# Weaving the bursts of two token pairs and moving three tiles' routing marks in a three-stage kernel

## The chip, the cores and the metric

The kernel runs on one core of a Trainium2 chip. The core has five engines with an instruction stream each: PE (TensorE, matrix products and transposes, with PEld its weight loads), DVE (VectorE), ACT (ScalarE), POOL (GpSimd) and SP (SyncE, which issues DMAs here). They run side by side and wait for each other on semaphores. The metric is the device time of one execution in microseconds (us); shown are the median, the lowest and the highest of several runs.

## The reference

Three layers follow each other: an attention with a window and block summaries, a dense mixture of four experts, and a mixture of eight experts in which each token goes to one expert at most and keeps its input beside it. There are 1536 tokens of 512 values, which the kernel holds as 12 tiles of 128 tokens.

```python
def _attn_ref(q, k, v):                    # q, k, v: (2, 8, 768, 64)
    block, window = (32, 16)
    k_sum = k.reshape(B, H, nb, block, D).max(axis=3)
    v_sum = v.reshape(B, H, nb, block, D).mean(axis=3)
    scores_l = scale * np.matmul(q, k.transpose(0, 1, 3, 2))
    mask_l = np.abs(pos[:, None] - pos[None, :]) < window
    scores_s = scale * np.einsum('bhsd,bhnd->bhsn', q, k_sum) + np.log(block)
    ...                                    # softmax over both, times v and v_sum

def _moe_ref(x, domain_probs, w1, w2):     # N, D, E, F = 1536, 512, 4, 1024
    p = domain_probs / (domain_probs.sum(-1, keepdims=True) + 1e-09)
    for e in range(E):
        h = np.maximum(x @ w1[e], 0.0)
        out += p[:, e:e + 1] * (h @ w2[e])

def _moe2_ref(x, w_skip, w_gate, w1, w2):  # E = 8
    do_compute = x @ w_skip > 0
    xc = x[do_compute]
    logits = xc @ w_gate
    e_idx = np.argmax(logits, axis=1)
    gate_w = probs[np.arange(len(xc)), e_idx]          # probs: softmax of logits
    y[mask] = gate_w[mask, None] * (np.maximum(xc[mask] @ w1[e], 0.0) @ w2[e])   # mask: e_idx == e
    out[do_compute] = xc + y
```

## The kernel before

**Stages.** From 0 to about 203 us run the attention and the first groups of the dense mixture, in an order that a scheduler makes. Then the order is the written one (`manual_schedule`, L1339): the function `middle` (L576) runs ten weight groups up to about 527 us; the last two groups run block by block up to 608 us (blocks of 4, 3, 3 and 2 token tiles), with the routing of the third layer between their products; and from there to the end the third layer runs in slots of 128 gathered tokens.

**Precision.** A product of full precision is built of three products of split values: each operand has a high part (cast) and a low part (what the cast left over), and high·high, high·low and low·high are summed in a PSUM bank. In names, `h` and `l` at the end are these parts. After the first matrix product `hh` is the relu of a bank, made by ACT, and `hl` its low part, made by DVE (L369, L370); both are needed by the second product (L382).

**The middle.** A weight group is a quarter of one expert's hidden width: 256 rows. The tokens are taken in two pairs of halves, pair "l" (tiles 4 to 11, 512 columns) and pair "s" (tiles 0 to 3, 256 columns). For each pair the 2×2 block product (weights by tokens) is made by seven products of sums instead of eight; each is a *burst* of six matmuls in one go (L509). They are called p1, p5, p6, p3, p7, p2, p4 and add up in three banks, with copies by ACT (the sums `u2` and `s5`) and additions by DVE (L544, L549) in between. Then the second product makes one *tile* of 128 tokens at a time (`second`, L560: six matmuls, then one DVE operation L570 onto the accumulator `acc`). Tiles are put into a list, `todo`, and one is taken from it behind nearly each burst; the list runs over into the next group. The table `at` (L583) says behind which burst the next group's weights are loaded, summed (POOL) and split (ACT casts, DVE subtractions). So a group has 14 bursts and 12 tiles.

**The routing.** `route_block` (L673) returns, for a block of token tiles, a list of routing steps and a list `place`. The steps store and transpose the block, make the logits, and `ranks` gives each token a place in its expert's list, which it counts on in `cum` (L752). In `place`, `places` *marks* (L759): a token's place is compared with all 640 places of the lists, one DVE operation per tile; `index` (L783) multiplies these marks with the token numbers and adds to `iacc` (L788). The steps go into a queue `rq` (L1413), and each small unit of the last groups' products pops one (L1404). What `rq` still holds is done in slot "x" with the last block's own list `r` (L1441): `slot_main` (L1040) takes one step behind each of its products (`step`). The last block's list contains its own `ranks`, `index(0, 1)` followed by the first gather, marks for the other places and the rest of `index`; behind these comes `first_trans` (L1437), which transposes the first gathered rows.

Of the kernel before, what the change touches and what calls it, by code (L numbers as in the profile page):

```python
# [19 lines left out]
P = 128  # L20
# [4 lines left out]
def attention_moe_kernel(  # L25
# [5 lines left out]
    B, S, _ = v.shape  # L31
    H, D = 8, q.shape[3]
    NT, DM = out.shape
    E1, NG, _, _ = w1.shape
# [13 lines left out]
    bank = [psp.tile([P, 512], F32, name=f"bank{i}") for i in range(8)]  # L48
# [357 lines left out]
    SGROUPS = range(4, E1 * NG - 2)  # L406

    PAIRS = {"l": (4 * P, 4 * P), "s": (0, 2 * P)}
    xsum, scr = {}, {}

    def x_quarter(p, i, j, c=slice(0, 2)):

        n0, n = PAIRS[p]
        return [x[:, 2 * i + c.start : 2 * i + c.stop, :] for x in x_at(n0 + j * n, n)]
# [39 lines left out]
    def w_steps(g):  # L454

        mid = g in SGROUPS

        def sums():
            raw = wtiles[g][0][0].rearrange("p (c f) -> p c f", c=KC)
            a11, a12, a21, a22 = (raw[:, 2 * j : 2 * j + 2, i * P : (i + 1) * P] for i in range(2) for j in range(2))  # L460
            t = scr["w"].tile([P, 3, 2, P], F32, name=f"ws{g}", tag="ws")
            tt = nc.gpsimd.tensor_tensor
            tt(out=t[:, 1], in0=a11, in1=a21, op=ALU.subtract)  # L463
            tt(out=a21, in0=a21, in1=a22, op=ALU.add)
            tt(out=t[:, 0], in0=a21, in1=a11, op=ALU.subtract)
            tt(out=t[:, 2], in0=a12, in1=t[:, 0], op=ALU.subtract)
            parts = [scr["w"].tile([P, 3, 2, P], F32R, name=f"ws{n}{g}", tag=f"ws{n}{g % 2}") for n in "hl"]
            wtiles[g] += [parts, t]

        def sum_parts(i):  # L470
            (h, l), t = wtiles[g][3:]
            s = slice(0, 2) if i == 0 else slice(2, 3)
            nc.scalar.copy(h[:, s], t[:, s])
            nc.vector.tensor_sub(l[:, s], t[:, s], h[:, s].bitcast(F32))  # L474

        no = lambda: None
        return [
            lambda: load_w(g), sums if mid else no, lambda: split_w(g, 1), lambda: split_w(g, 0),
            (lambda: sum_parts(0)) if mid else no, (lambda: sum_parts(1)) if mid else no,
            lambda: split_w(g, 2), lambda: split_w(g, 3),  # L480
        ]

    def pair_work(g, p, state_):

        n0, n = PAIRS[p]
        w1h, w1l = wtiles[g][1]
        wsh, wsl = wtiles[g][3]
        e = g // NG
        ba, be, bb = bank[state_["i"] % 2], bank[6], bank[7 - 2 * (state_["i"] % 2)]
        state_["i"] += 1  # L490
        hs, fs = {}, {}

        def wq(i, j):
            return [[w[:, (2 * j + c) * GF + i * P : (2 * j + c) * GF + (i + 1) * P] for w in (w1h, w1l)] for c in range(2)]

        def wsum(k):
            return [[w[:, k, c, :] for w in (wsh, wsl)] for c in range(2)]

        def xq(i, j):
            h, l = x_quarter(p, i, j)  # L500
            return [[x[:, c, :] for x in (h, l)] for c in range(2)]

        def xs(k):
            return [[x[:, k, c, :] for x in xsum[p]] for c in range(2)]

        def burst(b, w, x, start):
            for c in range(2):
                for i, (a, m) in enumerate(((0, 0), (0, 1), (1, 0))):
                    nc.tensor.matmul(  # L509
                        b[:, :n], w[c][a], x[c][m], start=start and c == 0 and i == 0, stop=c == 1 and i == 2,  # L510
                        skip_group_check=True,
                    )

        def tmp(nm):
            t = fs[nm] = scr["w"].tile([P, n], F32, name=f"{nm}{p}{g}", tag=f"{nm}{p}")
            return t

        def part(i, j, src):
            if p == "l" and j == 1:
                pool, tag = hp_, ("hh", "hl")  # L520
            else:
                pool, tag = scr["h"], (f"hh{p}{i}{j}", f"hl{p}{i}{j}")
            hh, hl = (pool.tile([P, n], F32R, name=f"{t}_{p}{g}_{i}{j}", tag=t) for t in tag)
            nc.scalar.activation(hh, src, AF.Relu)
            nc.vector.scalar_tensor_tensor(
                out=hl, in0=src, scalar=0.0, in1=hh.bitcast(F32), op0=ALU.max, op1=ALU.subtract,
            )
            hs[i, j] = (hh, hl)

        def p1():  # L530
            burst(ba, wq(0, 0), xq(0, 0), True)
            nc.scalar.copy(bb[:, :n], ba[:, :n])

        def p5():
            burst(be, wq(1, 0), xs(0), True)
            nc.scalar.copy(tmp("s5"), be[:, :n])

        def p6():
            burst(bb, wsum(0), xs(1), False)
            nc.scalar.copy(tmp("u2"), bb[:, :n])  # L540

        def p3():
            burst(be, wsum(2), xq(1, 1), False)
            nc.vector.tensor_add(fs["u2"], be[:, :n], fs["u2"])  # L544
            part(0, 1, fs["u2"])

        def p7():
            burst(bb, wsum(1), xs(2), False)
            nc.vector.tensor_add(fs["s5"], bb[:, :n], fs["s5"])  # L549
            part(1, 1, fs["s5"])  # L550

        def p2():
            burst(ba, wq(0, 1), xq(1, 0), False)
            part(0, 0, ba[:, :n])

        def p4():
            burst(bb, wq(1, 1), xs(3), False)
            part(1, 0, bb[:, :n])

        def second(j, t):  # L560
            w2h, w2l = wtiles[g][2]
            b = bank[2 + state_["b"] % 3]
            state_["b"] += 1
            for i in range(2):
                hh, hl = (h[:, t * P : (t + 1) * P] for h in hs[i, j])
                s = slice(i * DM, (i + 1) * DM)
                for k_, (a, w) in enumerate(((hh, w2h), (hh, w2l), (hl, w2h))):
                    nc.tensor.matmul(b, a, w[:, s], start=i == 0 and k_ == 0, stop=i == 1 and k_ == 2)  # L568
            t_ = n0 // P + j * (n // P) + t
            nc.vector.scalar_tensor_tensor(  # L570
                out=acc[:, t_, :], in0=b, scalar=pr[:, t_, e : e + 1], in1=acc[:, t_, :], op0=ALU.mult, op1=ALU.add,
            )

        return [p1, p5, p6, p3, p7, p2, p4], [lambda j=j, t=t: second(j, t) for j in (1, 0) for t in range(n // P)]

    def middle(todo):  # L576

        todo = list(todo)
        state_ = dict(i=0, b=0)

        wh = wtiles[SGROUPS[0]][1][0]
        nc.tensor.matmul(bank[7], wh[:, :P], wh[:, :512], start=True, stop=True)
        at = {0: (0,), 2: (1,), 4: (2,), 5: (3,), 7: (4,), 8: (5,), 9: (6,), 11: (7,)}  # L583
        for g in SGROUPS:
            nxt = w_steps(g + 1)
            i = 0
            for p in "ls":
                bursts, tiles = pair_work(g, p, state_)
                for b in bursts:
                    b()  # L590
                    for k_ in at.get(i, ()):
                        nxt[k_]()
                    if i not in (9, 12) and todo:
                        todo.pop(0)()
                    i += 1
                todo += tiles
        return todo


# [688 lines left out]
    rq = []  # L1288
    rstack, sstack, tstack = ExitStack(), ExitStack(), ExitStack()
    prev = None  # L1290
# [33 lines left out]
    for ch in chunks:  # L1324
        first = ch["ci"] == 0
        p1 = ch["gs"][0] < 2
        g = ch["g"]
# [10 lines left out]
        if ch["gs"] == (last - 1,) and first and ch["t0"] == 0:  # L1338
            ctx.enter_context(tc.manual_schedule())  # L1339
            prev = dict(gs=(last - 2,), last=True, b=middle(prev["b"]))  # L1340
            load_w(last)
# [65 lines left out]
        if prev is not None and prev["gs"][-1] == last and prev["last"]:  # L1407
            r, place = route_block(prev["t0"], prev["nt"])
            if prev["t0"] == 0:
                r += [None] * 4 + [early_pick] + [None] * 2 + [early_weights]  # L1410
            if prev["t0"] == 4:
                r += [None] * 3 + [early_list] + [None] * 3 + [early_gather, early_close]
            rq += r + [None] * 1 + place  # L1413
        prev = ch
    for f in prev["b"]:
        f()
# [21 lines left out]
        xts[0] = slot_trans("0", gat[0][2], bank[0])  # L1438

    r, place = route_block(prev["t0"], prev["nt"])  # L1440
    r = [f for f in rq if f is not None] + r  # L1441
    r += [None] * (FT - len(r)) + [first_trans]
    free += [rbp.tile([P, FF], F32, name=f"rb{i}") for i in range(NRB)]
    load_units(5)
# [96 lines left out]
```

## Time and profile before

| | |
|---|---|
| median of 3 runs | 708.9 us (708.82 to 712.36) |
| the profiled execution | 707.44 us, span in the trace 705.7 us |
| mean granted TensorE clock in it | 0.992 of full speed |
| busy share of the span | PE 97%, DVE 60%, ACT 35%, POOL 15% |
| DMA | 73.78 MB, mean 105 GB/s |

A busy share is a mean over stages with different limits. The profiled execution is one of its own and stands a little apart from the median; the rows in the section below are all from it. "Idle before" in brackets is how long an engine stood still ahead of an instruction, and behind the arrow stands what it was waiting for. A granted clock of 1.00 is full speed and 0.50 half of it.

### The profile page before, as it was taken

The page shows a single profiled execution, that of the slowest core. Times are in us where ns is not written, and L with a number is a line of the kernel's source. Part 1 is how long each engine was busy: PE and PEld are TensorE (multiplying, and loading weights), DVE is VectorE, ACT ScalarE, POOL GpSimd, SP SyncE. Part 2 cuts the span into 40 slices and gives each one's busy share as a digit, 9 for nine tenths or more (in the row PEclk, how much of TensorE's full clock was granted, in tenths as well). Part 3 has the DMA queues.
Part 4 walks back from the last instruction along what each step waited for, and adds up shares of the span by engine and source line. Part 5 has one row for each costly group of instructions (what it writes and reads, how often), then busy time and mean ns, then how long its engine had stood idle before and what let it go on. Part 6 is the DMA issues. An engine that isn't in the chain of part 4 may idle for free. (4 is left out here: it accounts for less than half of the span.)

```text
span 705.7 us, 10995 instructions
## 1 busy us (share of the span) xinstructions
PE 686.7 (97%) x4072; PEld 547.7 (78%) x4072; DVE 425.5 (60%) x1035; ACT 245.5 (35%) x617; POOL 103.5 (15%) x182
## 2 busy tenths in 40 slices
PE   7889999999999999999999999999999999899996
PEld 6879888878888888888888888888888888474361
DVE  7877664897437565565657565565654565584441
ACT  4656564532114232332323233332311223271240
POOL 6117200020001010101101010100010003331230
PEclk9999999999999999999999999999999999899999
DMA  9977210020000010000000010000050187467991
GB/s 260 262 174 163 65 47 23 31 90 30 31 0 31 31 60 30 31 31 30 31 31 33 27 60 30 31 31 30 31 211 0 61 338 269 154 245 293 413 406 40
DMA packets 39877, 73.78 MB, mean 105 GB/s; under 512 B 16740, under 2 KB 19812, under 8 KB 39824
## 3 DMA queue, kind: packets, MB, share of 16 engines
q1 hardware_dynamic: 38592, 70.31, 30.3%
q0 software_dynamic: 960, 2.25, 0.9%
q8 instruction: 32, 0.52, 0.3%
q10 hardware_dynamic: 272, 0.52, 0.2%
q14 instruction: 21, 0.17, 0.1%
HBM read 66.10 MB, written 7.86 MB: 105 GB/s over the span
## 5 line engine op out<-in xcount | busy, mean ns | idle before, releaser
L570 DVE SCALAR_TENSOR_TENSOR acc<-bank,pr,acc 128x512 f32<-128x512 f32 x120 | 89.7, 747 | 61.1 <-PE bank L568 60.9
L362 PE MATMUL bank<-xh,w1h 128*128 128x256 f32 (+2 forms) x208 | 68.6, 334 | 0.0
L362 PE MATMUL bank<-xl,w1h 128*128 128x256 f32 (+2 forms) x208 | 67.7, 326 | 0.0
L362 PE MATMUL bank<-xh,w1l 128*128 128x256 f32 (+2 forms) x208 | 67.4, 324 | 0.0
L382 PE MATMUL bank<-w2h,hh 128*128 128x512 f32 x144 | 58.7, 408 | 0.0
L382 PE MATMUL bank<-w2h,hl 128*128 128x512 f32 x144 | 54.6, 403 | 4.3 <-DVE hl L370 4.3
L382 PE MATMUL bank<-w2l,hh 128*128 128x512 f32 x144 | 56.8, 394 | 0.0
L463 POOL TENSOR_TENSOR ws<-raw 128x256 f32<-128x256 f32 x10 | 7.5, 753 | 335.2 <-DVE wsl L474 195.4
L370 DVE SCALAR_TENSOR_TENSOR hl<-bank,hh 128x256 fp32r<-128x256 f32 (+2 forms) x52 | 27.0, 520 | 45.3 <-ACT hh L369 45.2
L369 ACT ACTIVATE hh<-bank 128x256 fp32r<-128x256 f32 (+2 forms) x52 | 24.1, 463 | 86.2 <-PE bank L362 84.1
L294 ACT ACTIVATE sm<-sm,mn 128x120 f32<-128x120 f32 x96 | 36.7, 385 | 19.9 <-DVE mn L289 19.9
L362 PEld LDWEIGHTS bank<-xh,w1h 128*128 128x128 f32 x208 | 39.1, 189 | 4.3 <-DVE hl L370 0.4
L362 PEld LDWEIGHTS bank<-xl,w1h 128*128 128x128 f32 x208 | 39.4, 189 | 3.3
L362 PEld LDWEIGHTS bank<-xh,w1l 128*128 128x128 f32 x208 | 39.3, 189 | 2.6
L392 DVE SCALAR_TENSOR_TENSOR acc<-bank,pr,acc 128x512 f32<-128x512 f32 x43 | 30.0, 743 | 17.9 <-PE bank L382 17.9
L382 PEld LDWEIGHTS bank<-w2h,hl 128*128 128x128 f32 x144 | 26.8, 189 | 11.6 <-DVE hl L370 6.2
L382 PEld LDWEIGHTS bank<-w2h,hh 128*128 128x128 f32 x144 | 27.3, 190 | 6.4 <-issue 2.3
L568 PE MATMUL bank<-w2h,hhl_l 128*128 128x512 f32 x80 | 31.8, 397 | 0.0
L568 PE MATMUL bank<-w2l,hhs_s 128*128 128x512 f32 x80 | 31.7, 396 | 0.0
L568 PE MATMUL bank<-w2l,hhl_l 128*128 128x512 f32 x80 | 31.6, 396 | 0.0
L568 PE MATMUL bank<-w2h,hh_l 128*128 128x512 f32 x80 | 31.6, 395 | 0.0
L568 PE MATMUL bank<-w2l,hh_l 128*128 128x512 f32 x80 | 31.6, 395 | 0.0
(357 smaller groups left out, 1731.5 us busy)
## 6 DMA issues: line engine op xcount, KB each, us to landing
raw<-in_moe_w_dram SPq DMA_DIRECT2D x30, 512.0 KB, 3.2
ra<-in_moe_w_dram SPq DMA_DIRECT2D x27, 512.0 KB, 9.1
rb<-in_moe_w_dram SPq DMA_DIRECT2D x21, 512.0 KB, 8.6
acc<-in_moe_w_dram SPq DMA_DIRECT2D x15, 512.0 KB, 8.5
vwin<-in_v_dram SPq DMA_DIRECT2D x24, 192.0 KB, 3.3
kt<-in_k_dram SPq DMA_DIRECT2D x8, 384.0 KB, 6.2
qbd<-in_q_dram SPq DMA_DIRECT2D x24, 128.0 KB, 6.3
out_dram<-xg SPq DMA_DIRECT2D x12, 256.0 KB, 3.0
```

Of the source, the lines that this page charges most:

```text
L294: nc.scalar.activation(sm[:, h, :], sm[:, h, :], AF.Exp, bias=mn[:, h : h + 1], scale=-1.0, accum_out=su[:, h : h + 1],)
L362: nc.tensor.matmul(b[:, :n], wt[:, f0 : f0 + P], xt[:, c, :], start=(c == 0 and i == 0), stop=(c == KC - 1 and i == 2),)
L369: nc.scalar.activation(hh[:, :n], b[:, :n], AF.Relu)
L370: nc.vector.scalar_tensor_tensor(out=hl[:, :n], in0=b[:, :n], scalar=0.0, in1=hh[:, :n].bitcast(F32), op0=ALU.max, op1=ALU.subtract,)
L382: nc.tensor.matmul(bank[2 + t], ht[:, t * P : (t + 1) * P], wt[:, f0 : f0 + DM], start=(ci == 0 and i == 0), stop=(ci == nch - 1 and i == 2),)
L392: nc.vector.scalar_tensor_tensor(out=a, in0=bank[2 + t], scalar=sc, in1=a, op0=ALU.mult, op1=ALU.add,)
L463: tt(out=t[:, 1], in0=a11, in1=a21, op=ALU.subtract)
L568: nc.tensor.matmul(b, a, w[:, s], start=i == 0 and k_ == 0, stop=i == 1 and k_ == 2)
L570: nc.vector.scalar_tensor_tensor(out=acc[:, t_, :], in0=b, scalar=pr[:, t_, e : e + 1], in1=acc[:, t_, :], op0=ALU.mult, op1=ALU.add,)
```

## The change

In the middle, the fourteen bursts of both pairs are issued woven together by a table, `order`, instead of all of pair l and then all of pair s; the steps of the next group's weights are put behind other bursts, and the tiles of pair l's second half enter the list behind the eleventh burst. In the routing, `place` of tiles 7 to 9 is no longer put into `rq`: its two steps of marks and its `index` are put between the first steps of the last block, in slot "x".

```diff
@@ pair_work
-        ba, be, bb = bank[state_["i"] % 2], bank[6], bank[7 - 2 * (state_["i"] % 2)]
-        state_["i"] += 1
+        ba, be, bb = (bank[i] for i in ((0, 6, 7) if p == "l" else (1, 6, 5)))
@@ middle
-        at = {0: (0,), 2: (1,), 4: (2,), 5: (3,), 7: (4,), 8: (5,), 9: (6,), 11: (7,)}
+        at = {0: (0,), 2: (1,), 3: (2,), 5: (3,), 7: (4,), 9: (5,), 10: (6,), 12: (7,)}
+        order = ("l1", "l5", "s1", "l6", "l3", "s6", "l7", "s5", "l2", "s7", "l4", "s3", "s2", "s4")
         for g in SGROUPS:
             nxt = w_steps(g + 1)
-            i = 0
-            for p in "ls":
-                bursts, tiles = pair_work(g, p, state_)
-                for b in bursts:
-                    b()
-                    for k_ in at.get(i, ()):
-                        nxt[k_]()
-                    if i not in (9, 12) and todo:
-                        todo.pop(0)()
-                    i += 1
-                todo += tiles
+            work = {p: pair_work(g, p, state_) for p in PAIRS}
+            for i, (p, k) in enumerate(order):
+                work[p][0][k]()
+                for k_ in at.get(i, ()):
+                    nxt[k_]()
+                if i == 10:
+                    todo += work["l"][1][0]
+                for _ in range(2 if g == SGROUPS[0] and i < 2 else i not in (9, 10)):
+                    if todo:
+                        todo.pop(0)()
+            todo += work["l"][1][1] + work["s"][1][0] + work["s"][1][1]
@@ where a block's steps are queued
-            rq += r + [None] * 1 + place
+            if prev["t0"] == 7:
+                late = [f for f in place if f is not None]
+                rq += r
+            else:
+                rq += r + [None] * 1 + place
@@ ahead of slot x
-    r = [f for f in rq if f is not None] + r
+    r = [f for f in rq if f is not None] + r[:1] + late[:1] + r[1:2] + late[1:2] + r[2:3] + late[2:] + r[4:]
```

Where instructions move, three places are shown. The first is ACT in the first group of the middle: `hh_l_11` is made of what l7 gives, `hhl_l_10` of what l4 gives; `u2s`, `s5s` and `hhs` belong to pair s. The kernel before, and then the changed one:

```order
L524 ACTIVATE hh_l_01_2295<-u2l_2275 128x512
L524 ACTIVATE hh_l_11_2310<-s5l_2263 128x512
L101 CAST w1h_2247<-raw_0_2249 128x512
L524 ACTIVATE hhl_l_00_2322<-bank_61 128x512
L101 CAST w1h_2247<-raw_0_2249 128x512
L524 ACTIVATE hhl_l_10_2334<-bank_68 128x512
L532 COPY bank_66<-bank_62 128x256
```

```order
L523 ACTIVATE hh_l_01_2308<-u2l_2297 128x512
L539 COPY u2s_2318<-bank_66 128x256
L101 CAST w1h_2247<-raw_0_2249 128x512
L523 ACTIVATE hh_l_11_2329<-s5l_2267 128x512
L535 COPY s5s_2339<-bank_67 128x256
L473 CAST wsh_2289<-ws_2284 128x512
L523 ACTIVATE hhl_l_00_2349<-bank_61 128x512
L523 ACTIVATE hhs_s_11_2360<-s5s_2339 128x256
L473 CAST wsh_2289<-ws_2284 128x256
L523 ACTIVATE hhl_l_10_2372<-bank_68 128x512
```

Between the results of l7 and l4 stood only the weight casts and the result of l2; now there are also the copy of s5 and the result of s7.

The second is DVE at the end of the last groups: `ofs` and `cum` close the ranks of tiles 7 to 9, `sel` are their marks, and `hl_10_1` is the low part that the last two tiles' second product needs; `ls` are the last block's logits. Before, and then after:

```order
L748 SCALAR_TENSOR_TENSOR ofs<-ix_5499,r_5559 128x3
L752 TENSOR_TENSOR cum<-cum,oh_5502 128x8 x3
L759 TENSOR_SCALAR sel_5573<-iot,ofs 128x640 x3
L370 SCALAR_TENSOR_TENSOR hl_10_1_5592<-bank_62,hh_10_1_5591 128x256
L392 SCALAR_TENSOR_TENSOR acc<-bank_63,pr,acc 128x512
L788 TENSOR_TENSOR iacc<-iacc,bank_66 128x25
L392 SCALAR_TENSOR_TENSOR acc<-bank_64,pr,acc 128x512
L718 COPY ls_5690<-bank_66 128x18
```

```order
L750 SCALAR_TENSOR_TENSOR ofs<-ix_5499,r_5559 128x3
L754 TENSOR_TENSOR cum<-cum,oh_5502 128x8 x3
L370 SCALAR_TENSOR_TENSOR hl_10_1_5590<-bank_62,hh_10_1_5589 128x256
L392 SCALAR_TENSOR_TENSOR acc<-bank_63,pr,acc 128x512
L392 SCALAR_TENSOR_TENSOR acc<-bank_64,pr,acc 128x512
L761 TENSOR_SCALAR sel_5661<-iot,ofs 128x640 x3
L720 COPY ls_5677<-bank_66 128x18
```

The three marks stood between the additions to `cum` and `hl_10_1`; now they stand behind both additions to `acc`, ahead of `ls`.

The third is PE at the start of slot x: L1065 (L1067 after) are the slot's own products, L694 (L696) the last block's transposes, L700 (L702) and L710 (L712) its logits. Before, and then after:

```order
L1065 MATMUL bank_62<-ra_4758,acc 128x512
L694 MATMUL bank_67<-ident,acc 128x128 x4
L694 MATMUL bank_68<-ident,acc 128x128 x4
L1065 MATMUL bank_62<-ra_4759,acc 128x512
L700 MATMUL bank_67<-rxt_5647,wr 32x256 x4
L1065 MATMUL bank_62<-ra_4760,acc 128x512
L710 MATMUL bank_66<-fold,lt_5685 128x9 x2
L1065 MATMUL bank_62<-ra_4761,acc 128x512
L1065 MATMUL bank_63<-ra_4758,acc 128x512
```

```order
L1067 MATMUL bank_62<-ra_4758,acc 128x512
L696 MATMUL bank_67<-ident,acc 128x128 x4
L696 MATMUL bank_68<-ident,acc 128x128 x4
L1067 MATMUL bank_62<-ra_4759,acc 128x512
L1067 MATMUL bank_62<-ra_4760,acc 128x512
L702 MATMUL bank_67<-rxt_5627,wr 32x256 x4
L1067 MATMUL bank_62<-ra_4761,acc 128x512
L1067 MATMUL bank_63<-ra_4758,acc 128x512
L712 MATMUL bank_66<-fold,lt_5669 128x9 x2
L1067 MATMUL bank_63<-ra_4759,acc 128x512
```

Each of the two logit steps now comes one product of the slot later than the step before it, since a step of marks has taken a place.

## Rows read from the trace of the kernel before

**Rows 1.** The page, part 1: engine busy time, share of the span, instructions.
```profile
PE 686.7 (97%) x4072; PEld 547.7 (78%) x4072; DVE 425.5 (60%) x1035; ACT 245.5 (35%) x617; POOL 103.5 (15%) x182
```

**Rows 2.** Waits of the weight loads (PEld), 200 to 527 us: line, releaser, total, times, longest.
```profile
PEld bank L509 <- DVE s5l L549: 0.5, 1, 0.5
```

**Rows 3.** Waits of PE, 527 to 706 us.
```profile
PE bank L382 <- DVE hl L370: 3.2, 1, 3.2
PE bank L821 <- DVE cum L752: 0.2, 1, 0.2
```

**Rows 4.** Timeline of PE: start us, us, engine, line, operation, shapes, count [idle before].
```profile
216.08 0.40 PE L509 MATMUL bank<-xh,w1l 128*128 128x512 f32 x1
216.50 0.50 PE L509 MATMUL bank<-xslh,w1h 128*128 128x512 f32 x1
216.84 0.40 PE L509 MATMUL bank<-xsll,w1h 128*128 128x512 f32 x1
```

**Rows 5.** Timeline of PE around the wait for hl.
```profile
602.46 0.39 PE L382 MATMUL bank<-w2l,hh 128*128 128x512 f32 x1
606.08 0.80 PE L382 MATMUL bank<-w2h,hl 128*128 128x512 f32 x1 [3.24 <-DVE hl L370]
```

**Rows 6.** Timeline of ACT, copies to u2l of the second and tenth group.
```profile
237.35 0.59 ACT L540 COPY u2l<-bank 128x512 f32<-128x512 f32 x1 [2.14 <-PE bank L509]
...
489.40 0.59 ACT L540 COPY u2l<-bank 128x512 f32<-128x512 f32 x1 [2.14 <-PE bank L509]
```

**Rows 7.** Windows: A:B, length, busy us (x instructions) of PE, PEld, DVE, ACT, POOL, PEclk, DMA share, GB/s.
```profile
145.00:200.00 55.00, 54.98 (x242) 44.84 (x240) 37.06 (x58) 13.81 (x24) 6.70 (x8) 1.00 0.11 39
```

**Rows 8.** Timeline of DVE from ranks' additions on, and in slot x.
```profile
601.68 1.61 DVE L752 TENSOR_TENSOR cum<-cum,oh 128x8 bf16<-128x8 bf16 x3
603.22 2.48 DVE L759 TENSOR_SCALAR sel<-iot,ofs 128x640 bf16<-128x640 f32 x3
605.62 0.40 DVE L370 SCALAR_TENSOR_TENSOR hl<-bank,hh 128x256 fp32r<-128x256 f32 x1
...
615.01 0.18 DVE L718 COPY ls<-bank 128x18 f32<-128x18 f32 x1 [5.45 <-PE bank L710]
...
617.46 0.35 DVE L752 TENSOR_TENSOR cum<-cum,oh 128x8 bf16<-128x8 bf16 x2
```

**Rows 9.** Timeline of POOL beside the additions to cum.
```profile
602.00 1.28 POOL L999 TENSOR_TENSOR sl<-ra,sh 128x512 fp32r<-128x512 f32 x1 [1.81 <-ACT sh L998]
```

**Rows 10.** Windows around three waits of PE.
```profile
48.80:52.20 3.40, 3.40 (x27) 3.07 (x27) 2.95 (x14) 2.26 (x10) 0.18 (x1) 0.50 0.26 63
135.00:140.00 5.00, 3.96 (x22) 2.87 (x22) 5.00 (x10) 2.94 (x7) 0.00 (x0) 1.00 0.33 105
605.20:612.00 6.80, 5.92 (x30) 4.18 (x31) 2.42 (x5) 0.59 (x1) 1.43 (x3) 0.50 0.39 125
```

**Rows 11.** Timeline of PE, two earlier waits.
```profile
47.39 0.65 PE L316 MATMUL bank<-ident,sm 128*120 128x128 f32 x4 [1.97 <-DVE xl L338]
...
139.81 0.73 PE L382 MATMUL bank<-w2h,hl 128*128 128x512 f32 x2 [0.85 <-DVE hl L370]
```

**Rows 12.** Timeline of PE in slot x.
```profile
618.13 1.02 PE L1065 MATMUL bank<-ra,acc 128*128 128x512 f32 x2
618.99 0.20 PE L783 MATMUL bank<-code,sel 128*128 128x5 bf16 x2
...
624.21 0.60 PE L1025 MATMUL bank<-ident,xg 128*128 128x128 f32 x4
```

**Rows 13.** Timeline of POOL, issue of the first gather.
```profile
620.18 1.10 POOL L1011 DMA_INDIRECT xg<-out_dram,ixb  x1 [1.67 <-DVE ixb L812]
```

**Rows 14.** Answer on tile xg, 585 to 706 us, its last line.
```profile
DMA to landing us min/median/max: 3.4/5.9/6.7
```

More of the change, by code (lines that the diff above doesn't have):

```diff
@@ L572, in second @@
             )
-        return [p1, p5, p6, p3, p7, p2, p4], [lambda j=j, t=t: second(j, t) for j in (1, 0) for t in range(n // P)]
+        bursts = {"1": p1, "5": p5, "6": p6, "3": p3, "7": p7, "2": p2, "4": p4}
+        return bursts, [[lambda j=j, t=t: second(j, t) for t in range(n // P)] for j in (1, 0)]
     def middle(todo):
         todo = list(todo)
-        state_ = dict(i=0, b=0)
+        state_ = dict(b=0)
         wh = wtiles[SGROUPS[0]][1][0]
         nc.tensor.matmul(bank[7], wh[:, :P], wh[:, :512], start=True, stop=True)
-        at = {0: (0,), 2: (1,), 4: (2,), 5: (3,), 7: (4,), 8: (5,), 9: (6,), 11: (7,)}
+        at = {0: (0,), 2: (1,), 3: (2,), 5: (3,), 7: (4,), 9: (5,), 10: (6,), 12: (7,)}
+        order = ("l1", "l5", "s1", "l6", "l3", "s6", "l7", "s5", "l2", "s7", "l4", "s3", "s2", "s4")
         for g in SGROUPS:
             nxt = w_steps(g + 1)
-            i = 0
-            for p in "ls":
-                bursts, tiles = pair_work(g, p, state_)
-                for b in bursts:
-                    b()
-                    for k_ in at.get(i, ()):
-                        nxt[k_]()
-                    if i not in (9, 12) and todo:
+            work = {p: pair_work(g, p, state_) for p in PAIRS}
[7 more added lines that the diff above has]
+                    if todo:
                         todo.pop(0)()
-                    i += 1
-                todo += tiles
+            todo += work["l"][1][1] + work["s"][1][0] + work["s"][1][1]
         return todo
```

## Prediction

> **What bounds the kernel now.** I read the page's busy shares first, then the waits of PE stretch by stretch, then the timelines around each wait. The shares show one engine full and the rest with room [rows 1]: PE is busy 97% of the span, DVE 60%, ACT 35%, POOL 15%. So the end is PE's own work plus whatever PE waits for. In the middle (200 to 527 us) the only wait is one of 0.5 us, a weight load held for DVE's addition to s5l [rows 2]. From 527 us to the end one wait stands out: an L382 product waits 3.2 us for DVE's hl [rows 3]. Two more things cost PE time without being a wait: the pace of the products in the middle, and a stretch behind that 3.2 us wait where the clock is halved. The change touches these four places and no other, since the first 203 us are issued as before.
>
> **Part one, the weave: first group.** Before, the first group runs out of leftover products, so l4 is issued one burst behind l7 while DVE still adds to s5l. The starts show it: 216.08, 216.50 and 216.84 [rows 4], so distances of 0.42 and 0.34 us where two products of 512 columns in a row stand 0.23 apart (602.23 to 602.46 [rows 5]); that is 0.30 us, the rest of the 0.5 lies at the same spot of the s pair. After, s5, l2 and s7 stand between l7 and l4: two bursts of six 256-column products and one of six 512-column ones, 12 × 0.12 + 6 × 0.23 = 2.8 us, and the addition is long done. Gain 0.5 us, at least 0 and at most 0.5.
>
> **Part one: later groups.** The bursts, the products behind them and the additions are the same in number. What can change is the distance from a burst that writes a bank to the burst that needs what DVE or ACT made of it. In the order before, the shortest was a product tile and one s burst (1.4 + 0.7 = 2.1 us, s5 to s3) and no group but the first shows a wait; after, the shortest such distance is l4, s3, a tile, s2 and a tile (s7 to s4), 5.6 us. The weight preparation, moved by a burst or two, is work of ACT, DVE and POOL, which have 65%, 40% and 85% of their time free; if that cover were gone it would show as a wait of tenths of a us in each of ten groups. I cost it at nothing.
>
> **Part one: pace.** A group takes 31.51 us: the copy to u2l starts at 237.35 in the second group and at 489.40 in the tenth, 252.05 / 8 [rows 6]. It holds 42 products of 512 columns and 42 of 256 in bursts and 72 of 512 in tiles, worth 135 of 512 columns. A uniform stretch issued 242 products in 55.00 us, 0.2273 each [rows 7]; 135 × 0.2273 = 30.7 us. So the middle runs 0.83 us a group above that pace, 8.3 us over ten groups, without a wait to show for it. I don't know the cause, and the weave mixes the widths more finely: from −8.3 (all of it goes) to +8.3 (as much again). The set of products and of operands stays the same, so I take 0.
>
> **Part two, the marks out of the way of hl.** Here lies most of the sum. PE could go on at 602.69 (602.46 + 0.23) and goes on at 606.08 [rows 5]. It waits for hl, which DVE starts at 605.62; ahead of it DVE has the three additions to cum (601.68, 1.61 us) and the three marks of tiles 7 to 9 (603.22, 2.48 us) [rows 8]. After, hl stands right behind cum (second pair of orders above): it starts when the marks did, at 603.22 or a little earlier, and PE goes on 0.46 us behind that start as it does now (605.62 to 606.08), at 603.68. Gain 606.08 − 603.68 = 2.4. The additions to cum could end earlier: three of them take 1.61 us here and two take 0.35 at 617.46 [rows 8]; next to the slow ones POOL runs a subtraction from 602.00, for 1.28 us [rows 9], and in the new order the cast on ACT that it waits for comes one place sooner. I take 2.5, between 2.1 (the casts slip instead) and 3.2 (the whole wait of [rows 3]).
> The Trainium skill ("SBUF — State Buffer", section "SBUF: two separate sides") says that DVE and GpSimd share a pair of ports under an exclusive lock, so that a DVE operation with two SBUF inputs stands still until a GpSimd operation that was first has finished. The cum additions are of that kind and the trace agrees: 1.61 us beside POOL's subtraction, 0.35 without. By that rule the new order can't bring PE on before POOL's subtraction is over, and the gain stays at 2.4 to 2.7; without it, cum would end near 602.2 and the whole 3.2 would be gained.
>
> **Part two: the clock.** Behind the wait the granted clock was 0.50 from 605.2 to 612.0, with 5.92 us of PE work in it [rows 10]: the 1.2 GHz level, where the rest of the kernel has 2.4. At full clock this work takes 2.96 us, so 2.95 us are lost. An earlier case is alike: PE idles 1.97 us before 47.39 [rows 11] and the clock is 0.50 over 48.8 to 52.2 [rows 10]. Against it stands a wait of 0.85 us before 139.81 [rows 11], with 1.00 granted over the 5 us ahead of it [rows 10] and over the 55 us behind it [rows 7]. After, PE waits about 1 us (602.69 to 603.6), nearer to 0.85 than to 1.97. So I take the clock as staying up: gain 2.95, and 0 at the other end.
>
> **Part two: what the marks now cost.** They move between the last block's steps in slot x, 2.48 us of DVE work. DVE idles 5.45 us before 615.01 there [rows 8], which hides them; if that cover were gone, up to 2.5 us would be late at the first gather. The index products of tiles 7 to 9 are moved, not added: 0.
>
> **Part two: the first gather.** Two things shift in slot x: the first list's index comes two products later and the transposition of what it gathers one product later. So one product less lies between, 0.86 us (618.13 to 618.99 [rows 12]). Now the gather is issued at 620.18 [rows 13]; the gathers landed 3.4, 5.9 and 6.7 us (least, median, most) behind their issue [rows 14], and this one was used at 624.21 [rows 12], so it landed within 4.0, with at most 0.63 us to spare over the least. After, 0.23 us of a wait appears at the least, and two more DVE operations stand ahead of the issue. I take 0.5; the ends are 0 and, with a landing at 6.7 instead of 3.4, 3.3 more. SP's weight loads behind the last index are reached some 4.5 us earlier on the whole and wait for buffers as before: 0.
>
> **Sum.** −0.5 (first group) − 2.5 (marks) − 2.95 (clock) + 0.5 (gather) = −5.45. The profiled execution took 707.44 us (span 705.7 and 1.74 around it), so it becomes 702.0. The median of the runs shown, 708.9, is 1.46 above that execution, so the forecast is 703.4. Its own range, with the marks' ends, the first group's, and a gather's wait of 0 to 1.5 us, is 702.2 (−6.65) to 705.3 (−3.55).
>
> **Rivals.**
> *The clock falls all the same*, at this wait or at the gather's. Then the sum is −2.5: 706.4. For it: a wait of a third remains. Against: the 0.85 us before 139.81 cost no clock.
> The Trainium skill ("TensorE: Matmul & The Clock Gate", Part 1, "What's actually happening") has it that the clock's watch is not tied to the start of a kernel, so that the same kernel changes clock at different points from run to run. By that, a short wait could still meet a fall in some runs, and this case's time would be seen in these; no run so far shows it here.
> *The first gather lands late*: its 3.3 us more make a wait longer than the 1.97 us after which the clock was seen to fall, so about 2.95 come on top: 703.4 + 2.8 + 2.95 = 709.2. For it: the median landing of 5.9. Against: the same gather landed within 4.0.
> *Slower: the weave makes a wait in each group.* Place: s5 and s3 use the bank that l5 and l3 use, so s5 now waits for DVE's addition behind l3, and DVE's additions come in bunches between the 0.75 us ones of the tiles and the weight preparation. Price: ten groups times the wait. At 1 us a group it is 703.4 + 10 = 713.4; from 0.55 a group it eats the whole gain. For it: the woven order brings the two closer than before. Against: between l3 and s5 stand two bursts and three tiles, over 6 us, and DVE is free for 40%.
> *The pace of the middle changes*, by up to 8.3 us: 695 to 711.7, either sign.
>
> **Chances.** Forecast 0.73, clock 0.11, late gather 0.07, wait per group 0.05, pace 0.04. A difference of 0.5%, 3.5 us, is about what a measurement of this kernel can tell from no change: faster is below 705.4, slower above 712.4. Faster: 0.73 and half of the pace's, 0.75. Slower: the wait per group and a quarter of the pace's, 0.06. The rest, 0.19, within. The range 701.5 to 706.6 takes in the forecast and the clock's case, and 0.7 us below its best end, for a pace a little better.
>
> **What would show it.** Right: no L509 wait in the middle and a group of 31.5 us; hl directly behind cum; PE's wait there near 1 us; the granted clock at 1.00 from 600 to 615 us; a wait of some tenths before the transposition of the first gathered rows. Wrong: a clock of 0.50 behind 603 us or behind the gather, a wait for DVE or ACT in every group, a gather wait above 1.5 us, a group period other than 31.5.

## The result

Changed kernel: median 701.4 us of 10 runs (700.28 to 706.38); the kernel before beside it 708.9 us of 10 (706.7 to 712.36). The ratio is 0.9911, 95% interval 0.9888 to 0.9935: 6.3 us less, between 4.6 and 7.9. Forecast were 703.4 us, that is −5.45, with a range from 701.5 to 706.6; the median lies 0.1 us under that range. The two medians stand 7.5 us apart, which lies within the interval. In a second comparison (below) the ratio was 0.9923 (0.9897 to 0.9950).

The page of the changed kernel, part 1 (answers to [rows 1]), its PE waits from 520 to 700 us ([rows 3]), and the one wait of a weight load for gathered rows, 600 to 640 us:

```profile
PE 683.6 (98%) x4072; PEld 545.6 (78%) x4072; DVE 425.7 (61%) x1035; ACT 244.7 (35%) x617; POOL 102.8 (15%) x182
```
```profile
PE bank L382 <- DVE hl L370: 0.6, 1, 0.6
PE bank L823 <- DVE cum L754: 0.2, 1, 0.2
```
```profile
PEld bank L1027 <- DMA xg<-out_dram,ixb: 0.4, 1, 0.4
```

The span fell from 705.7 to 699.1 us. PE's busy time fell by 3.1 us though not one product is gone: products at half clock take nearly twice as long (0.42 us from start to start in L382 behind the wait, 607.72 to 608.14, where 0.23 is usual). From 200 to 527 us the view lists no wait any more, of PE or of its weight loads ([rows 2] had one).

Four landmarks of PE cut a run into stages: the first burst product (L509, L508 after), the last product of the middle's tiles, the first and the last of the slots' own products (L1065, L1067 after); what follows is 6.97 us in every trace, to 0.01. Taken from the starts in each trace, in us:

| kernel (one profiled execution each) | first burst at | middle | last two groups | slots |
|---|---|---|---|---|
| before | 203.17 | 322.89 | 82.50 | 90.18 |
| changed | 202.39 | 322.13 | 78.31 | 89.27 |
| changed, again | 203.73 | 322.13 | 78.31 | 89.28 |
| weave only | 204.09 | 322.13 | 82.81 | 89.53 |
| routing only | 206.47 | 322.68 | 78.63 | 89.34 |
| marks back | 203.76 | 322.13 | 82.51 | 91.47 |
| 13 products in the wait | 204.97 | 322.68 | 82.70 | 90.30 |
| 20 products in the wait | 204.28 | 322.93 | 82.50 | 89.68 |
| zeros by ACT | 204.76 | 322.68 | 80.53 | 88.94 |
| cast later | 207.79 | 322.13 | 79.13 | 89.28 |
| ranks late | 205.33 | 322.13 | 77.15 | 89.85 |

The first column is a stage that no kernel here changes, and it moves by 5.4 us. The others repeat: to 0.01 us in the two executions of the changed kernel, and in the middle to 0.25 over the five kernels with the old order of bursts. So mechanisms are read from the other columns, and only the timed ratios say what a kernel is worth. Between the two first rows lie −0.78 (not the change), −0.76, −4.19 and −0.91 us; the three stages that the change touches lost 5.86 us together, where −5.45 was forecast.

The place of the big term, in the changed kernel, on PE, DVE and POOL ([rows 5], [rows 8], [rows 9]), and windows behind it ([rows 10]):

```profile
600.85 0.39 PE L382 MATMUL bank<-w2l,hh 128*128 128x512 f32 x1
601.80 0.50 PE L382 MATMUL bank<-w2h,hl 128*128 128x512 f32 x1 [0.56 <-DVE hl L370]
```
```profile
599.74 1.67 DVE L754 TENSOR_TENSOR cum<-cum,oh 128x8 bf16<-128x8 bf16 x3
601.33 0.42 DVE L370 SCALAR_TENSOR_TENSOR hl<-bank,hh 128x256 fp32r<-128x256 f32 x1
...
603.70 1.47 DVE L761 TENSOR_SCALAR sel<-iot,ofs 128x640 bf16<-128x640 f32 x3
```
```profile
599.90 1.29 POOL L1001 TENSOR_TENSOR sl<-ra,sh 128x512 fp32r<-128x512 f32 x1 [1.87 <-ACT sh L1000]
601.13 2.39 POOL L1431 MEMSET xg<- 128x512 f32 x5
```
```profile
604.00:608.00 4.00, 4.00 (x22) 1.88 (x21) 1.17 (x3) 1.96 (x4) 1.27 (x1) 1.00 0.94 269
608.00:612.00 4.00, 4.00 (x36) 2.38 (x35) 2.02 (x17) 1.40 (x3) 0.42 (x3) 1.00 0.96 375
```

PE goes on 0.95 us behind the product ahead, so it waits 0.72 (0.95 − 0.23) where it waited 3.39. hl is right behind the additions to cum, these still take 1.67 us beside POOL's subtraction, and end just behind it. The clock is 1.00. The marks run later, in 1.47 us for all three: look at that number again below.

### The profile page after: what moved, and what is told of

The parts are those of the page before. It is cut to its first block, busy times and chain, and to the rows that moved or that the text cites. A ratio compares the mean times of both kernels' runs of the same rounds, so it can differ in the third digit from the quotient of the medians.

```text
span 699.1 us, 10979 instructions
## 1 busy us (share of the span) xinstructions
PE 683.6 (98%) x4072; PEld 545.6 (78%) x4072; DVE 425.7 (61%) x1035; ACT 244.7 (35%) x617; POOL 102.8 (15%) x182
## 5 line engine op out<-in xcount | busy, mean ns | idle before, releaser
L382 PE MATMUL bank<-w2h,hh 128*128 128x512 f32 x144 | 58.3, 405 | 0.0
L382 PE MATMUL bank<-w2l,hh 128*128 128x512 f32 x144 | 56.5, 393 | 0.0
L382 PE MATMUL bank<-w2h,hl 128*128 128x512 f32 x144 | 54.1, 399 | 1.6 <-DVE hl L370 1.6
L102 DVE TENSOR_TENSOR w1l<-raw,w1h 128x512 fp32r<-128x512 f32 x30 | 20.6, 690 | 22.4 <-ACT w1h L101 22.3
L382 PEld LDWEIGHTS bank<-w2h,hl 128*128 128x128 f32 x144 | 26.5, 188 | 8.8 <-DVE hl L370 3.6
L382 PEld LDWEIGHTS bank<-w2h,hh 128*128 128x128 f32 x144 | 27.2, 189 | 6.5 <-issue 2.3
L567 PE MATMUL bank<-w2h,hll_l 128*128 128x512 f32 x80 | 31.8, 397 | 0.0
```

The costliest lines, as they stand in the source:

```text
L102: nc.vector.tensor_sub(wl[:, s], r, wh[:, s].bitcast(F32))
L382: nc.tensor.matmul(bank[2 + t], ht[:, t * P : (t + 1) * P], wt[:, f0 : f0 + DM], start=(ci == 0 and i == 0), stop=(ci == nch - 1 and i == 2),)
```

## The experiments

"Before" in a verdict is the kernel before, run beside it on the same chip. The time lost to the clock is worked out as (1 − mean granted clock) × span, averaged over a kernel's runs; it holds the falls of the whole run, also those of the first 65 us and of the last 1 to 4 us.

**Weave only.** The changed kernel with the two routing edits taken back.
```diff
-            if prev["t0"] == 7:
-                late = [f for f in place if f is not None]
-                rq += r
-            else:
-                rq += r + [None] * 1 + place
+            rq += r + [None] * 1 + place
-    r = [f for f in rq if f is not None] + r[:1] + late[:1] + r[1:2] + late[1:2] + r[2:3] + late[2:] + r[4:]
+    r = [f for f in rq if f is not None] + r
```


> Only the woven bursts; the marks and the index of tiles 7 to 9 are queued as before. Theory (nearly all of the gain is the wait for hl and the clock behind it): 708.9 - 0.5 to 0.8 = 708.1 to 708.4 us, the wait for hl is 3.2 us as before and the granted clock behind it 0.50 for some 6.8 us; no wait in the middle. Rival (the weave carries the gain, by its pace): under 705 us.

Measured: 707.65 us, ratio 0.9988 (0.9964 to 1.0013). The middle is 322.13, as in every woven kernel, against 322.68 to 322.93 in every other: the weave is worth 0.55 to 0.80 us, and the rival falls. Its waits, and DVE and POOL there:

```profile
PE bank L382 <- DVE hl L370: 3.9, 1, 3.9
```
```profile
601.43 1.67 DVE L754 TENSOR_TENSOR cum<-cum,oh 128x8 bf16<-128x8 bf16 x3
603.02 3.46 DVE L761 TENSOR_SCALAR sel<-iot,ofs 128x640 bf16<-128x640 f32 x3
606.40 0.41 DVE L370 SCALAR_TENSOR_TENSOR hl<-bank,hh 128x256 fp32r<-128x256 f32 x1
```
```profile
601.60 1.29 POOL L1001 TENSOR_TENSOR sl<-ra,sh 128x512 fp32r<-128x512 f32 x1 [1.88 <-ACT sh L1000]
602.83 2.39 POOL L1427 MEMSET xg<- 128x512 f32 x5
```

Here the marks take 3.46 us and the wait is 3.9, not 2.48 and 3.2. The order is that of before; what differs is that POOL's memsets began 0.2 us ahead of the marks here (602.83 and 603.02). In the kernel before they began together with them (603.22, [rows 8]) and themselves took longer:

```profile
603.22 3.42 POOL L1425 MEMSET xg<- 128x512 f32 x5
```

The granted clock fell behind the wait here too, to 0.90, 0.50 and 0.75 in the three windows from 606 to 612 us: 3.4 us at half clock, where 6.8 were expected.

```profile
608.00:610.00 2.00, 2.00 (x5) 1.19 (x5) 0.98 (x3) 0.00 (x0) 0.00 (x0) 0.50 0.25 35
```

**Routing only.** The kernel before with the two routing edits.
```diff
-            rq += r + [None] * 1 + place
+            if prev["t0"] == 7:
+                late = [f for f in place if f is not None]
+                rq += r
+            else:
+                rq += r + [None] * 1 + place
-    r = [f for f in rq if f is not None] + r
+    r = [f for f in rq if f is not None] + r[:1] + late[:1] + r[1:2] + late[1:2] + r[2:3] + late[2:] + r[4:]
```


> Only the marks and the index of tiles 7 to 9 moved; the bursts in the order of before. Theory: 701.4 + 0.5 to 0.8 = 701.9 to 702.2 us, the wait for hl about 0.6 us, granted clock 1.00 behind it, the 0.5 us wait of the first group back. Rival (the weave carries the gain): over 705 us.

Measured: 704.73 us, ratio 0.9927 (0.9901 to 0.9952), where the expected 701.9 to 702.2 us are 0.9902 to 0.9906 of the 708.9: inside the interval, at its lower edge. In absolute time it is 2.5 to 2.8 us off; the first stage, 206.47 in the profiled execution, may have its share. The clock is as expected, the first group's wait of 0.5 us is back, and the wait for hl is 0.3 us longer:

```profile
PE bank L382 <- DVE hl L370: 0.9, 1, 0.9
```
```profile
606.00:608.00 2.00, 1.25 (x5) 1.05 (x6) 1.41 (x4) 0.00 (x0) 2.00 (x5) 1.00 0.00 0
608.00:610.00 2.00, 2.00 (x12) 1.26 (x11) 2.00 (x5) 0.73 (x2) 0.67 (x2) 1.00 0.59 174
```

**Marks back.** The changed kernel; only the marks return to their old place, the index stays in slot x.
```diff
-                late = [f for f in place if f is not None]
-                rq += r
+                marks = [f for f in place if f is not None]
+                late = [None, None, marks[2]]
+                rq += r + [None] * 1 + [marks[0], None, marks[1]]
```


> The changed kernel with the three marks put back into the queue as before, so ahead of hl; the index of tiles 7 to 9 stays in slot x, all steps there keep their places. Theory: the 3.2 us wait and the half clock come back: 701.4 + 2.6 + 2.9 = 706.9 us. Rival (the index moved off the last groups, or the order in slot x, gives the gain): 701 to 703 us.

Measured: 707.93 us, ratio 0.9976 (0.9950 to 1.0003): most of the gain is lost again. The last two groups are back at 82.51, with the wait and the half clock:

```profile
PE bank L382 <- DVE hl L370: 3.9, 1, 3.9
```
```profile
606.00:608.00 2.00, 1.47 (x4) 1.18 (x5) 1.11 (x3) 0.00 (x0) 0.00 (x0) 0.50 0.00 0
608.00:610.00 2.00, 2.00 (x4) 0.87 (x3) 0.87 (x2) 0.00 (x0) 0.00 (x0) 0.50 0.37 92
610.00:612.00 2.00, 2.00 (x10) 1.89 (x9) 0.00 (x0) 0.59 (x1) 0.00 (x0) 0.50 1.03 346
```

So it is the marks ahead of hl, not the index and not the order in slot x.

**13 products in the wait.** The kernel before, with idle work for PE.
```diff
+                if i == 2 and t0 == 10 and gs[0] > 1 and ci == nch - 1 and t == 0:
+                    for _ in range(13):
+                        nc.tensor.matmul(bank[4], hh[:, :P], wh[:, f0 : f0 + DM], start=True, stop=True)
```


> The kernel before, with 13 products of 512 columns (3.0 us, into a bank that nothing reads) put ahead of the product that waits for hl: PE works through the wait instead of standing still. Theory (the clock falls because PE stands still): the wait is 0.2 to 0.5 us, the granted clock stays at 1.00 from 602 to 612 us, and the time is 708.9 - 2.9 = 706.0 us although no work was taken away. Rival (the clock falls there for another reason, the load of DMA or of the other engines): 0.50 again, 708.9 us.

Measured: 707.83 us, ratio 0.9964 (0.9940 to 0.9989): faster by 0.8 to 4.3 us, with 13 products more. But the trace of its profiled execution doesn't show what was expected: the marks, begun within 0.01 us of the memsets, took 3.65 us there, a wait of 1.5 us was left, and the clock fell behind it.

```profile
604.79 2.39 POOL L1428 MEMSET xg<- 128x512 f32 x5
604.80 3.65 DVE L762 TENSOR_SCALAR sel<-iot,ofs 128x640 bf16<-128x640 f32 x3
```
```profile
PE bank L385 <- DVE hl L370: 1.5, 1, 1.5
```
```profile
608.00:610.00 2.00, 1.16 (x18) 0.96 (x19) 1.41 (x3) 0.00 (x0) 0.00 (x0) 1.00 0.00 0
612.00:614.00 2.00, 2.00 (x9) 1.75 (x8) 0.00 (x0) 0.93 (x2) 0.00 (x0) 0.50 1.03 348
```

Over its 12 runs 4.1 us are lost to the clock against 6.1 over the 31 runs of before, more than the spread of the runs explains (2.0, with some 0.9 either way): the clock stays up more often, not always.

**20 products in the wait.** The same with `range(20)`.

> The kernel before, with 20 unused products (4.5 us) ahead of the product that waits for hl, where 13 left a wait of 1.5 us. Theory (the clock falls because PE stands still): no wait for hl is left, the clock is 1.00 from 600 to 620 us, mean granted clock 0.995 or more; the time is 706 to 707 us, some 2 to 3 under the kernel before in the same call, with up to 0.6 us of the products lying behind hl. Rival (another cause): 0.50 again behind this place, mean clock 0.991, no gain.

Measured: 707.48 us, ratio 0.9992 (0.9974 to 1.0009). No wait for hl is left and the clock is 1.00 all the way:

```profile
606.00:608.00 2.00, 2.00 (x10) 1.65 (x9) 1.16 (x3) 0.00 (x0) 1.77 (x3) 1.00 0.00 0
608.00:610.00 2.00, 2.00 (x23) 1.46 (x22) 0.94 (x3) 0.00 (x0) 0.00 (x0) 1.00 0.00 0
610.00:612.00 2.00, 2.00 (x12) 1.21 (x10) 0.65 (x1) 0.81 (x2) 0.00 (x0) 1.00 0.65 188
```
```profile
603.77 4.70 PE L384 MATMUL bank<-w2h,hh 128*128 128x512 f32 x20
608.30 0.39 PE L385 MATMUL bank<-w2h,hl 128*128 128x512 f32 x1
...
624.76 0.44 PE L1028 MATMUL bank<-ident,xg 128*128 128x128 f32 x2 [0.93 <-DMA xg<-out_dram,ixb]
```

In this execution the clock's part is as expected; over the runs 3.9 us are lost to it against 5.2 of before, a difference of 1.3 that is no larger than its own uncertainty. The time is not as expected: the products end 1.1 us behind hl, which was there at 607.2, and slot x waits 0.93 us for the first gathered rows. These two give back 2.0 us of what the clock brought; the last two groups and the slots together are 0.5 us shorter than before.

**Zeros by ACT.** The kernel before, its five gather buffers cleared by ACT instead of POOL.
```diff
-        nc.gpsimd.memset(t, 0.0)
+        nc.scalar.mul(t, rt["iot"][:, :DM], 0.0)
```


> The kernel before, with the five buffers of gathered rows set to zero by ACT and not by POOL. Theory (the three marks are held by POOL's memsets): the marks take 1.5 us, as in slot x, in place of 2.5 to 3.6; the wait for hl is 2.0 to 2.2 us in place of 3.2 to 3.9; some 1 to 2 us of gain, more where the clock stays up. Rival (the marks cost what they cost): 2.5 us or more, a wait of 3.2 or more, 708 to 709 us.

Measured: 705.93 us, ratio 0.9987 (0.9959 to 1.0014), so the time alone doesn't tell. The trace does:

```profile
603.07 1.61 DVE L752 TENSOR_TENSOR cum<-cum,oh 128x8 bf16<-128x8 bf16 x3
604.60 1.47 DVE L759 TENSOR_SCALAR sel<-iot,ofs 128x640 bf16<-128x640 f32 x3
605.99 0.41 DVE L370 SCALAR_TENSOR_TENSOR hl<-bank,hh 128x256 fp32r<-128x256 f32 x1
```
```profile
PE bank L382 <- DVE hl L370: 2.2, 1, 2.2
```
```profile
606.00:608.00 2.00, 1.54 (x20) 1.26 (x21) 1.24 (x4) 0.00 (x0) 0.00 (x0) 1.00 0.03 8
```

With POOL idle the same marks take 1.47 us in the same place. Two fifths of what I had costed as the marks' own work was POOL's memsets. And behind a wait of 2.2 us the clock stayed at 1.00. That gives the fall's price: PE's order is that of before, and from the product that waited to the first slot product behind the transposes PE took 5.90 us before (606.08 to 611.98) and takes 3.24 here, 2.66 less.

```profile
606.46 0.50 PE L382 MATMUL bank<-w2h,hl 128*128 128x512 f32 x1 [2.24 <-DVE hl L370]
...
609.70 1.02 PE L1065 MATMUL bank<-ra,acc 128*128 128x512 f32 x2
```

**Cast later.** The changed kernel, POOL's subtraction moved away from the additions to cum.
```diff
-                if ch["t0"] == 10 and ch["gs"][0] == last - 1 and micro_ % PRE == PRE - 1:
+                if ch["t0"] == 10 and ch["gs"][0] == last - 1 and micro_ % PRE == PRE - 2:
```


> The changed kernel with the split steps ahead of slot x put one product unit earlier in the count, so that the last cast on ACT, and with it POOL's subtraction, comes behind hh of the last product and no longer beside the three additions to cum. Theory (the additions to cum are held by POOL's subtraction): they take about 0.5 us in place of 1.6, the wait for hl goes from 0.7 us to 0, and the time is 0.5 to 0.9 us under the changed kernel's. Rival (they are slow of themselves, three in a chain): 1.6 us again and the wait stays at 0.6 to 0.9.

Measured: 704.74 us, ratio 0.9958 (0.9941 to 0.9976), not better than the changed kernel. Half of the theory holds, DVE and POOL:

```profile
602.21 1.25 DVE L777 CAST code<-gr 128x3 bf16<-128x3 f32 x1
603.49 1.19 DVE L779 TENSOR_TENSOR gr<-gr,code 128x3 f32<-128x3 f32 x1
...
606.08 1.09 DVE L750 SCALAR_TENSOR_TENSOR ofs<-ix,r 128x3 f32<-128x3 uint32 x1
607.10 0.55 DVE L754 TENSOR_TENSOR cum<-cum,oh 128x8 bf16<-128x8 bf16 x3
```
```profile
602.13 2.53 POOL L1001 TENSOR_TENSOR sl<-ra,sh 128x512 fp32r<-128x512 f32 x2 [4.04 <-ACT sh L1000]
605.86 1.29 POOL L1001 TENSOR_TENSOR sl<-ra,sh 128x512 fp32r<-128x512 f32 x1 [1.20 <-ACT sh L1000]
```

The additions take 0.55 us, so they are not slow of themselves. But POOL's subtraction now holds the operation ahead of them, `ofs`, for 1.09 us in place of 0.16, and a wait of 0.7 us stays. Ahead of that, POOL has two subtractions in a row where the changed kernel has one; they hold a cast of 3 columns for 1.25 us, as there, and now also the operation behind it for 1.19, and PE gets a second wait for hl, of 0.40. The hold was moved, not removed.

**Changed kernel again**, for comparison with the three above.

> The changed kernel once more, on the same chip as the three others, for comparison: ratio to the kernel before 0.991, mean granted clock of its runs 0.995, wait for hl 0.6 to 0.9 us. If the gain were a matter of the chip or of one sample: a ratio of 0.996 or more.

Measured: 702.80 us, ratio 0.9923 (0.9897 to 0.9950), an interval that leaves out the 0.996 of the rival; a wait for hl of 0.6 us, 3.6 us lost to the clock where before lost 5.2, and the same stages to 0.01 us.

**Ranks late.** The changed kernel, with the ranks of tiles 7 to 9 moved too.
```diff
                 late = [f for f in place if f is not None]
-                rq += r
+                late[0] = lambda f=r[-1], m=late[0]: (f(), m())
+                rq += r[:-1]
```


> The changed kernel with the ranks of tiles 7 to 9 (three small products each, the additions to cum) moved behind the last blocks too, into slot x ahead of their marks: on DVE hl then stands right behind the hl before it, and no operation that POOL can hold stands ahead of it. Theory (what is left of the wait is DVE's queue ahead of hl): no wait of PE between 527 and 610 us, the stretch from the middle's end to slot x 0.6 to 1.0 us shorter than the changed kernel's 78.31, of which the moved small products (0.3 us) come back in slot x; the time is 0.3 to 1 us under the changed kernel's, a ratio to the kernel before of 0.989 to 0.992, and the mean granted clock 0.995 or more. Rival (the routing in slot x is by now late enough to hold the first gather): a wait for xg or sel of 0.5 us or more in slot x that eats it, ratio 0.993 or more.

Measured: 701.23 us, ratio 0.9882 (0.9861 to 0.9902): faster than before by 7.0 to 9.9 us. Its waits from 520 to 660 us, and DVE's two hl:

```profile
PE bank L1027 <- DMA xg<-out_dram,ixb: 0.3, 1, 0.3
PE bank L823 <- DVE cum L754: 0.2, 1, 0.2
```
```profile
601.72 0.42 DVE L370 SCALAR_TENSOR_TENSOR hl<-bank,hh 128x256 fp32r<-128x256 f32 x1
602.76 0.43 DVE L370 SCALAR_TENSOR_TENSOR hl<-bank,hh 128x256 fp32r<-128x256 f32 x1 [0.63 <-ACT hh L369]
```

hl waits for nothing but ACT's hh. Against the changed kernel the last two groups lose 1.16 us and the slots get 0.58 back, 0.3 of it PE's wait for the first gathered rows (the weight load ahead of it waits 0.8): 0.58 us better in the traces. The timed ratios of the two overlap, so that it beats the changed kernel is shown by the stages alone, one trace of each. The mean clock of its 5 runs is 0.994, not the 0.995 expected: 3.9 us lost against 6.1 of before.

## Why the prediction was right, point by point

- **First group, −0.5.** Right: −0.55 to −0.80 in the middle, no wait left; 0.2 of it is the next point, so the first group has 0.4 to 0.6. That part of the old wait lay in the s pair is not shown: [rows 2] lists one wait, for s5l.
- **Later groups and pace, 0.** Right but for a trifle: six woven kernels have 322.13 us, to the hundredth, and no wait came. The pace moved by 0.02 us a group: the copies to u2l of the second and the tenth group start at 235.35 and 487.24, so a group takes 31.49 us, not 31.51; 0.2 us over nine groups.
- **Marks out of the way of hl, −2.5.** Right in the execution it was worked out from: 3.39 − 0.72 = 2.67. But it was one execution with a short wait: the same order gave 3.9 us in two others, so the step is worth up to 0.7 us more. What I took for 2.48 us of marks is 1.47 of marks and the rest POOL's memsets, which I had in no row.
- **DVE held by POOL.** Here the rule of the Trainium skill ("SBUF — State Buffer", "SBUF: two separate sides") that I weighed was borne out: 1.67 us of additions beside the subtraction, 0.55 without, and with the order changed the hold goes to other small operations (`ofs`, a cast). It doesn't go to all: in ranks late hl, which has a PSUM bank as an input, ran beside the subtraction (602.52 to 603.82) in its usual 0.43 us. The hold also reached further than I had applied it: the marks and the memsets hold each other as well.
- **Clock, −2.95.** Right in kind in the profiled pair (0.50 over 6.8 us, then 1.00); the same instructions measured at either level give 2.66 (zeros by ACT). As a mean it is smaller: the kernels with the long wait lose 5.2 to 6.5 us a run to the clock, the changed one 3.2 and 3.6. Against the kernel before run beside it that is 1.6 us (5.2 to 3.6), and 2.2 for routing only (6.1 to 3.9).
- **Clock, the reason.** A long wait is what brings the fall, or the lack of work in it: with 13 products in it less is lost over the runs, with 20 no fall came in the one profile. But its length alone doesn't decide: 3.2 and 3.9 us (before, weave only, marks back) brought one in 3 of 3 profiles, 0.9 or less in none of 6 (with 20 products in it, too), and between them 1.5 us did and 2.2 did not. My reading, "nearer to 0.85 than to 1.97", came out, on a border that isn't there as a line. The first 60 us of the same traces, where PE waits often, agree: weave only has four waits of 1.63 to 1.78 us there and keeps 1.00 from 7 us on, and in ranks late, routing only and cast later the clock fell behind waits of 1.73, 1.88 and 1.93.
- **Index moved at no cost.** Right as a sum: it left the last groups and came into the slots. That is why the slots gained only 0.91 us where the 3.4 us at half clock that had lain in them (608.57 to 612.0 [rows 10]) were worth 1.7; 0.1 of the difference is the first gather, and no run separates the index from the new order of the steps in the rest.
- **First gather, +0.5.** Too large. The weight load waited 0.4 us, but most of that beside the product that PE was at: this one and the first transposition start 0.33 us apart (617.75 and 618.08) where they stood 0.24 apart before (623.97 and 624.21), so PE lost 0.1. In the second execution the load waited 0.2 us and PE lost nothing (0.23 apart).
- **The absolute time.** 2.0 us under the forecast. The step that failed is the base: I carried over as fixed that the median lies 1.46 us above the profiled execution. For the changed kernel that gap is 0.58 (701.37 and 700.79), which makes 0.9 of the 2.0; another 0.8 is the first stage of the execution, shorter by 0.78 with the code unchanged, and 0.4 is the three stages that the change touches (−5.86 for −5.45). What makes the gap to the median is not shown, as only profiled executions have stages; a first stage that moves by 5.4 us can do it. The difference, −5.45, lies within the interval of both comparisons (4.6 to 7.9 and 3.5 to 7.3 us).
- **Rivals.** The late gather, the wait per group and the pace didn't come; the clock fell in neither of the two profiles of the changed kernel behind this place, but for the last 2.3 and 1.5 us of the run. That the same kernel changes clock at different points from run to run is seen in these two: their first fall is at 48 us in one and at 13 in the other. A fall behind the short wait in some other run is not ruled out.

What stays open: which of the changed kernel's runs lose the clock and where (only profiled executions show the place), and why 1.5 us cost it once where 2.2 did not.

## What to carry to other kernels

Where PE is full, look for the one long wait and for what stands ahead of the releaser in its engine's queue; moving that behind work which nobody waits for is worth the wait and, at times, the clock behind it. Before an operation is costed by its duration in a trace, see whether GpSimd ran beside it: the same three marks took 1.47, 2.48 and 3.46 us, and 3.65 once. And take a forecast's base from many runs, its differences from stages.

## What the runs showed of the hardware that I had not expected

- DVE's marks (128 x 640, a bf16 result of an f32 input) and POOL's memsets slow each other: marks 1.47 us alone, 3.46 with the memsets 0.2 us ahead (these then 2.39). Where both began within 0.01 us it went either way: 2.48 in the kernel before [rows 8] and 2.49 with 20 products in the wait, with 3.42 and 3.43 for the memsets, but 3.65 with 13 products, with 2.39 for the memsets.
- POOL's subtraction of 1.28 us holds very small operations of DVE as well: 0.16 to 1.09 us for one of 3 columns, 0.17 to 1.25 for a cast of 3. It did not hold hl (128 x 256, with a PSUM bank as an input): 0.43 us beside it in ranks late.
- The granted clock fell behind a wait of PE of 1.5 us and not behind one of 2.2, with much the same work around them, in one execution each.
